# One product with the unit matrix replaced by a subtraction on GpSimd, and a new order of all steps, in a local attention with a gated feed-forward kernel

## The chip, the cores and the metric

One core of one Trainium2 chip runs the whole program. The metric is the device time of one execution in microseconds (us), and the lower the better. The kernel before took 375.93 us, the median of three runs (375.56 to 376.45). For this kernel a difference of under about 0.2%, some 0.75 us, can't be told from none.

## The reference

The input is `q`, `k`, `v` of 4 batches, 8 heads, 768 positions and 64 features, in float32. The positions are cut into 24 chunks of 32. Each chunk of queries sees 8 memory keys and its own neighbourhood:

```python
for c in range(nc):
    l_start, r_end = max(0, c_start - 16), min(S, c_end + 8)
    k_full = np.concatenate([mem_k, k[:, :, l_start:r_end]], axis=2)
    v_full = np.concatenate([mem_v, v[:, :, l_start:r_end]], axis=2)
    scores = scale * np.matmul(q_c, k_full.transpose(0, 1, 3, 2))
    a = np.exp(scores - np.max(scores, axis=-1, keepdims=True))
    a = a / (np.sum(a, axis=-1, keepdims=True) + 1e-09)
    out[:, :, c_start:c_end] = np.matmul(a, v_full)
```

The result, 4 x 768 x 512, goes through a feed-forward block whose gate mixes positions:

```python
h = gelu_tanh(x @ w_in)                      # 512 -> 1024
u, v = h[..., :512], h[..., 512:]
v_n = (v - mean(v)) / sqrt(var(v) + 1e-06) * g_ln
v_s = np.einsum('ts,bsd->btd', w_sg, v_n) + b_sg[None, :, None]
return x + (u * v_s) @ w_out
```

## The kernel before, in words

**High and low parts.** Every float32 factor of the large products is split into a part `hi`, which TensorE takes as it is, and a rest `lo = value - hi`. A product is then three products: lo times hi, hi times lo, hi times hi. The weights arrive as 64-bit words; `weight_steps` turns one piece of 128 x 512 into float32 in steps `r` (transfer, SyncE), `d3` (ScalarE), `d2`, `d5`, `d6` (VectorE), rounds it to `hi` in `d8` (ScalarE) and makes `lo` in `d9`. For most pieces `d9` is a subtraction on GpSimd (or VectorE). For the pieces of `w_in` named in `BY_TENSOR`, TensorE makes it: step `X` multiplies the piece by the unit matrix and subtracts `hi` by a product with the negative unit matrix, and `d9` is then a copy out of PSUM on ScalarE. The pieces are named by half and row block: `i10` to `i13` make the second half of `w_in` (for `v`), `i00` to `i03` the first (for `u`).

**Stages.** An attention unit `u` (24 of them, 6 for each batch, 128 positions each) is loaded by `q`, `k`, `v` (SyncE), scored by `S` (TensorE), and goes through `mx` (row maxima, VectorE), `sb` (subtract them, VectorE), `ex` (exp, ScalarE), `z` (clear absent keys, GpSimd), `sm` and `sr` (sum, reciprocal, VectorE), `nm` (normalise, VectorE or, starred, GpSimd), `T` (transpose, TensorE), `p` (copy out of PSUM, ScalarE or, starred, VectorE), `A` (times the values, TensorE), `xc` and `xh` (ScalarE) and `xl` (VectorE or GpSimd), which leave the unit's hi and lo part. Then `V` (batch, unit) multiplies by the second half of `w_in`, and `U` (batch, half, block) by the first, each with three times four or more matmuls. `v1`, `u1` are the gelu, `v5`, `vx`, `vy`, `v6`, `v7` the normalisation; `W`, `O` are the gate product and `w_out` for batches 0 and 1. Batches 2 and 3 use a form with fewer products, with steps `M` and `N`, whose weights (sums of blocks of `w_sg`, made earlier and kept in device memory by `ys`) come back by `yr` and `yq` into room that the attention buffers held before.

**The order.** Nothing loops: the text `ORDER` names every step once, and each step issues its instructions on its engine in the place where it stands there. So `ORDER` fixes the instruction stream of each of the five engines; an engine takes its own stream strictly in turn, and semaphores hold an instruction until its operands are there and its buffer is free. A star chooses a step's second engine. `zz8` and `zz4` are matmuls with the unit matrix whose result nobody reads. Four PSUM buffers `mma` to `mmd` are handed out in the order in which they come free (`mms`), to `X`, `T`, `V`, `U`, `W`, `O`, `M` and `N` alike. In the trace all helpers record one line, L107, so one reads by buffer names: `ea` to `ed` hold the scores of four units, `pt` the transposed ones, `paira` and `pairb` hi and lo of the two halves of a batch, `ma` to `mh` the weight pieces while they are made (`mb` is i11, `mf` i01, `mg` i02, `mh` i03), `raw` what was loaded for them.

At the start TensorE runs, in step names: `zz8 S0 zz4 S1 Xi10 zz8 S2 T0 S3 Xi12 T1 A0 Xi11 S4 Xi13 A1 T2 S5 T3 V01 A2 V00 S7 S6 V02 U000`.

Of the kernel before, what the change touches and what calls it, by code (L numbers as in the profile page):

```python
# [39 lines left out]
ri00 zz4 d6i10 mx0 S1 k3 q3 d3i12 d2i12 d5i12 d8i10 Xi10 sb0 mx1 sb1 ex0 v0 ri02 q4 k4 zz8 v1 z0 sm0 sr0 nm0 d6i12  # L40
d3i03 ex1 d2i03 S2 sm1 T0 d9i10 d3i00 S3 p0* sr1 nm1* d2i00 mx2 mx3 sb2 sb3 d8i11 d8i12 Xi12 d9i12 T1 A0 Xi11 ex2 q5
k5 ex3 S4 d3i02 d8i13 xc0 p1 xh0 Xi13 d9i13 d5i00 sm2 sr2 d6i00 mx4 nm2* q6 sm3 sr3 d5i03 sb4 A1 d9i11 xh1 v2 ri01 T2
S5 q7 k7 xl1 d6i03 k6 d8i00 d8i03 p2 ex4 xl0 mx5 d3i01 nm3* T3 V01 A2 ro0 V00 v5 d9i00 sb5 d2i02 d5i02 d9i03* d2i01
xh2 ex5 S7 v100 d5i01 d6i02 d6i01 d8i01 xl2 d8i02 xc1 d9i01* S6 z5 v101 sm5 sm4 v3 g00 v501 vx01 sr5 mx6 p3* sr4 vy01
d3o0 xc2 k9 V02 d2o0 sb6 d9i02 mx7 sb7 q9 nm5* ex6 U000 v601 v4 v701 nm4* T5 A3 U002 xc3 p5 T4 g50 g20 g10 S9 k11 v6
ex7 v500 g40 g21 k8 xh3 v801 A5 z6 p4 vx00 vy00 sm7 sm6 v901* v102 u1002 ga50 v600 v700 A4 xc4 xc5 v800 v502 xl3 sr6
d5o0 d6o0 xh5 v900* gb50* xl5* U003 V03 d8o0 xh4 xl4* ga20 ga00 vx02 vy02 d9o0* u1000 ga40 gb40* V05 ga10 v103 ga21
v503 v105 nm6* v602 mx9 vx03 gb20 U001 v505 vy03 sb9 ex9 sm9 v702 vx05 V04 gb00 gb10 v603 q8 ro2 g31 g30 q11 g11 T6
v703 ga30 gb30* sr7 nm7* vy05 p6* cg S11 g41 S8 ro1 ga31 u1001 v605 v705 q10 v802 U010 mx8 v803 v902 v104 u1003 ga11
k10 gb21 v504 vx04 vy04 v604 v704 sb8 v805 v905* v903* gb11 v804 v904 U012 U011 T7 S10 A6 p7* sr9 d3o1 u1010 gb31* cb  # L50
u1012 d3o2 ex8 xc6 ga41 mx11 d2o1 d5o1 W003 d2o2 sb11 d5o2 nm9* d6o1 k12 g51 W001 W002 ga51 ex11 w1003 w2003 k13 w3003
d8o1 v9 mx10 w1001 gb41 w4003 gb51 w1002 sb10 w2002 sm8 q12 q13 g01 W000 w1000 d6o2 d9o1* sr8 w2000 ga01 gb01 W012
w1012 ro3 d3o3 d2o3 d5o3 w2012 w2001 v7 T9 d8o2 ex10 w3002 w3000 z11 nm8* d6o3 S13 S12 k15 q14 q15 v8 k14 A7 xc7 u1011
mx12 W010 w4002* T8 d8o3 w4000 W011 d9o2* w1010 sb12 w2010 sm11 p9* sr11 sm10 w1011 w2011 mx13 sb13 U013 w3001 w4001
d9o3 ea1 ex12 u1013 p8 ea2 sr10 ex13 nm10* ea3* eh1 O003 O001 nm11* sm13 o1001 w3010 w4010 el1* O000 O002 v10 yl000
yl010 yl110 yl100 yc10 o1000 eb1 es1 eb2* o1003 xh7 eh2 xh6 w3012 w3011 ed1* xl7* T11 S14 S15 W013 w1013 w4012* w2013
T10 A9 p11* A8 w4011 V11 p10 xc8 el2 xl6* V10 mx14 w3013 v111 xh8 xc9 w4013 O012 xl8 es2 z12 v110 v511 sr13 o1002 ed2
mx15 v510 o1012 nm13* sm12 sr12 vx10 vy10 eh4 el4 O010 O011 sb15 nm12* vx11 sb14 vy11 v611 v711 v811 v911 v610 yc30*
ex15 v710 o1010 yc20* T12 k17 v12 k16 v11 A11 A10 o1011 ec1 ec2 ex14 sm14 sr14 p12* v810 es4 q16 v13 q17 V12 O013 v112
v512 sm15 ec3* xc10 xc11 eh3 xh10 U102 U101 u1102 xl10 el3 T13 S17 S16 V14 xh11 v910* o1013 sr15 nm15* xl11* xh9 vx12  # L60
vy12 mx17 sb17 k18 xl9* q18 es3 v14 V15 v612 v114 p13 v514 mx16 v712 out002 v812 T15 A13 A12 v115 yc40* v912 yh50 vx14
vy14 v515 ym50 p15* sb16 v614 V13 ys50 out012 k19 out003 q19 out000 ex16 v113 U111 U100 U103 vx15 vy15 nm14 v714 v615
v715 v815 u1101 v915 v513 vx13 yh60 yh40 v814 vy13 v613 v914* yl001 v713 ym40* yh70 T14 S19 S18 mx18 u1111 U113 ym70
v813 u1103 ys70 ys40 v913 sb18 ex17 ex18 u1100 W101 u1113 ym60 W111 W103 v15 yl011 z17 p14* w1101 w2101 mx19 sm17
w3101 w1103 W102 ys60 out001 w4101 w1111 k20 yl111 sr17 w2111 sm16 w2103 yc11* yc31* sr16 yc21 sb19 nm16 yh71 ym71*
W113 yh61 xc12 w3103 ex19 nm17* yh51 U110 z18 sm18 u1110 ym51 q20 k21 q21 yl101 w1102 w2102 w3102 w4102* U112 out011
ys51 w3111 xc13 W100 w1100 w2100 u1112 sr18 w1113 w2113 w3113 w4103* nm18 yc41* T17 S20 S21 W112 w1112 w2112 mx20 mx21
W110 sm19 w1110 w2110 w4113* T16 yl002 q22 k22 ys71 yh41 w3112 w3100 sb20 w3110 w4111* sb21 sr19 nm19 A15 A14 ym61 q23
yl012 out013 ym41 yr50 w4112 w4100 O100 p17 o1100 O101 O102 w4110 O103 xh12 xc14 o1101 p16* O111 O113 o1111 out010
xc15 ex21 out100 yl112 v17 yl102 v16 o1102 T18 A17 A16 O110 out101 v18 ys41 k23 ys61 xh13 yc12* yh52 xh14 xl14* ex20  # L70
sm20 yc32* yc22* yc42* ym52 yh62 o1103 out103 out102 ys52 sr20 p18* yh42 xc17 sm21 ym62* xl12 T19 p19* nm20* o1110
o1113 S22 S23 O112 mx22 xl13* o1112 V20 T20 ys62 v19 xc16 xh16 ym42* A19 A18 ys42 out111 yr51 V22 xh17 sb22 xl16* ex22
yh72 ym72 ys72 sm22 V21 xc19 xh15 sr21 nm21* xl15 v122 xl17 V24 v20 out113 v22 out110 yr52 v121 v522 db* v521 vx21
vy21 vx22 v124 vy22 v622 mx23 v120 v722 v520 V23 v21 vx20 vy20 v721 T21 p21* sb23 v524 v620 out112 v123 xc18 v523 sr22
ex23 U203 V25 p20 v720 nm22 vx23 v723 U202 v621 vz20 vz22 vy23 z23 vz21 v125 u1202 vx24 vy24 sm23 T22 A21 u1203 A20
xc20 v525 vx25 sr23 p22* v725 sh21 v624 v724 vz24 xc21 nm23* v623 vy25 v625 vz25 vz23 U213 U211 T23 A22 p23 v23 A23
yr71 yr60 c12 sl21* U201 u1201 sh22 u1213 c32 sh25 u1211 yr62 yr61 er4 yr70 c22 U200 u1200 sh26 sl26 M210 sl22* M221
M211 yr72 c42 mr211 mr210 M220 sl25 mr220 M261 M260 mr221 sh27 mr261 M251 sl27 md21 mr251 w2201* mr260 md20* w2200
# [808 lines left out]
```

## Time and profile before

| | |
|---|---|
| median of three runs | 375.93 us |
| the profiled execution | 375.81 us |
| its span, first to last instruction | 374.0 us |
| mean granted TensorE clock | 0.989 of full speed |
| busy: TensorE, VectorE, ScalarE, GpSimd | 361.4, 259.2, 179.1, 148.1 us |

The profiled execution lies 0.12 us below the median, and 1.81 us of it lie outside the span. An engine's busy time says little by itself here: TensorE is at work nearly all the time, so the places to read are the few in which it waits, and what it waits for. The rows below come from the page, from the list of who waited for whom, from the timeline of single engines, and from the list of what touched one buffer.

### The profile page before, as it was taken

The numbers are of one execution on the slowest core, as the hardware profiler recorded it, in microseconds if no ns is written. First come the engines' busy times: TensorE is split into PE (matmuls) and PEld (weight loads), VectorE is DVE, ScalarE is ACT, GpSimd is POOL, SyncE is SP. The second block draws the span as 40 slices with busy tenths as digits, with TensorE's granted clock in tenths as the row PEclk, the third lists the DMA queues.
The fourth block names the chain that finished last, engine by engine and source line by source line (L and its number), as shares of the span: only waits on it lengthen the run. The fifth ranks groups of instructions, "written<-read, shape, count | busy, mean of one in ns | idle before, by whom it ended". The sixth has DMA issues, their size and how long they took to land.

```text
span 374.0 us, 11057 instructions
## 1 busy us (share of the span) xinstructions
PE 361.4 (97%) x4762; PEld 333.3 (89%) x4762; DVE 259.2 (69%) x474; ACT 179.1 (48%) x306; POOL 148.1 (40%) x160
## 2 busy tenths in 40 slices
PE   4989999999999999999999999999999999999995
PEld 1457998999999998999999998899999889999995
DVE  3988986886874676644558281845355986988896
ACT  3556797563644382681711633674133543533340
POOL 1031434743255656453224525221825525115161
PEclk9799999999999999999999999999999999999999
DMA  7978867481913523765237969115528030224005
GB/s 296 381 274 309 320 206 230 116 271 78 328 66 119 219 86 122 244 243 174 70 87 237 340 227 336 50 58 159 198 83 268 27 87 1 86 84 147 2 0 189
DMA packets 30496, 63.76 MB, mean 170 GB/s; under 512 B 3568, under 2 KB 16624, under 8 KB 30448
## 3 DMA queue, kind: packets, MB, share of 16 engines
q1 hardware_dynamic: 30448, 63.06, 49.7%
...
q14 instruction: 11, 0.09, 0.1%
...
## 4 chain that ended last, share of the span: by engine, by line
PE 92%; DMA 3%; DVE 1%; issue 1%; SPq 1%; ACT 0%; DVEq 0%; ACTq 0%
PE mma L107 26%; PE mmc L107 21%; PE mmb L107 19%; PE mmd L107 15%; PE av L107 7%; PE s L107 4%; DMA qa<-in_qs 2%; DMA qb<-in_qs 1%; SPq L107 1%; DVE pt L107 0%; DVE vn L107 0%; DVE stats L107 0%; DVE rda L107 0%; ACT eb L107 0%; ACT vn L107 0%
## 5 line engine op out<-in xcount | busy, mean ns | idle before, releaser
L107 ACT ACT_TABLE_LOAD x24 | 30.8, 1283 | 7.0 <-DVE ec L107 2.6
L107 ACT CAST vh<-vn 128x768 fp32r<-128x768 f32 (+1 forms) x26 | 19.0, 738 | 26.2 <-PE mmd L107 10.5
L107 POOL TENSOR_TENSOR vh<-vn,vh 128x512 fp32r<-128x512 f32 (+1 forms) x11 | 17.2, 1569 | 32.7 <-ACT vh L107 32.6
L107 DVE BATCH_NORM_STATS2 stats<-vn 128x6 f32<-128x512 f32 x24 | 16.4, 688 | 18.7 <-ACT vn L107 18.6
L107 POOL TENSOR_TENSOR stats<-stats,mhalf 128x1 f32<-128x1 f32 x24 | 15.5, 648 | 28.3 <-DVE stats L107 28.3
L107 PE MATMUL mma<-w_sg_hi,vh 128*128 128x384 f32 x102 | 21.5, 337 | 0.0
L107 DVE TENSOR_TENSOR vh<-vn,vh 128x768 fp32r<-128x768 f32 (+1 forms) x15 | 16.3, 1098 | 4.6 <-ACT vh L107 4.6
L107 PEld LDWEIGHTS mma<-w_sg_hi,vh 128*128 128x128 f32 x102 | 17.9, 188 | 0.1
L107 PE MATMUL mmb<-w_sg_hi,vh 128*128 128x384 f32 x66 | 13.8, 336 | 0.8 <-DVE pt L107 0.8
L107 PEld LDWEIGHTS s<-ka,qa 64*32 64x32 f32 x704 | 8.2, 109 | 7.0 <-issue 6.5
L107 PE MATMUL s<-ka,qa 64*32 64x64 f32 x704 | 10.0, 232 | 4.5 <-DMA qa<-in_qs 4.0
L107 PE MATMUL mmc<-w_sg_hi,vh 128*128 128x384 f32 x66 | 13.9, 337 | 0.0
L107 DVE TENSOR_SCALAR vn<-vn,stats 128x512 f32<-128x512 f32 x12 | 9.5, 791 | 5.1 <-POOL stats L107 5.0
L107 PEld LDWEIGHTS mmb<-w_sg_hi,vh 128*128 128x128 f32 x66 | 11.6, 188 | 0.9 <-DVE pt L107 0.9
L107 PEld LDWEIGHTS s<-kb,qb 64*32 64x32 f32 x768 | 8.7, 109 | 3.9 <-issue 1.8
L107 PE MATMUL mmd<-w_sg_hi,vh 128*128 128x384 f32 x54 | 11.6, 335 | 0.0
L107 PEld LDWEIGHTS mmc<-w_sg_hi,vh 128*128 128x128 f32 x66 | 11.5, 188 | 0.1
L107 DVE SCALAR_TENSOR_TENSOR mma<-mma,g_all,b_all 128x384 f32<-128x384 f32 x6 | 3.8, 626 | 11.2 <-PE mma L107 11.2
L107 PE MATMUL s<-kb,qb 64*32 64x64 f32 x768 | 10.6, 232 | 0.8 <-DMA qb<-in_qs 0.8
L107 ACT ACTIVATE vn<-mmc 128x512 f32<-128x512 f32 x8 | 4.8, 597 | 13.7 <-PE mmc L107 11.8
L107 PE MATMUL mma<-pairb,w_in_hi 128*128 128x384 f32 x56 | 10.9, 335 | 0.0
L107 PE MATMUL mma<-w_sg_lo,vh 128*128 128x384 f32 x51 | 10.6, 335 | 0.0
...
## 6 DMA issues: line engine op xcount, KB each, us to landing
...
```

The source lines that it names most:

```text
L107: return self.tc.keep_in_program_order(getattr(self.engine, name)(*args, **kw))
```

## The change

One name leaves the list of pieces whose low part TensorE makes, so that the low part of piece `i11` becomes a GpSimd subtraction `w_in_lo<-mb,w_in_hi`; step `Xi11`, with its three matmul records, and the copy out of PSUM on ScalarE are gone. All steps of `ORDER` stand in a new order, of which two lines are shown:

```diff
-BY_TENSOR = ("i10", "i11", "i12", "i13")
+BY_TENSOR = ("i10", "i12", "i13")
...
-ri11 d3i11 d2i11 d5i11 ri10 d3i10 d2i10 d6i11 k0 zz8 ri13 d5i10 q0 d3i13 S0 k1 q1 ri12 d2i13 d5i13 d6i13 ri03 k2 q2
+ri11 ri13 d3i13 d3i11 d2i13 d5i13 d6i13 zz8 d2i11 d5i11 d6i11 d8i11 ri10 q0 q1 k0 q2 ri00 d3i10 S0 mx0 sb0 d2i10 d5i10
```

TensorE's stream now begins: `zz8 S0 zz4 S1 zz8 T0 S2 S3 Xi10 A0 T1 Xi12 A1 Xi13 S4 S5 T2 V00 T3 A2 V01 S6 S7 V02 U003`.

The first transfers on SyncE, in the order of issue, before (`raw` buffers are pieces of `w_in`; the two `vn` are keys and queries of unit 2):

```order
L107 DMA rawb<-in_w_in 128x1024
L107 DMA rawa<-in_w_in 128x1024
L107 DMA ka<-in_ks 128x736
L107 DMA rawd<-in_w_in 128x1024
L107 DMA qa<-in_qs 128x512
L107 DMA kb<-in_ks 128x736
L107 DMA qb<-in_qs 128x512
L107 DMA rawc<-in_w_in 128x1024
L107 DMA rawh<-in_w_in 128x1024
L107 DMA vn<-in_ks 128x736
L107 DMA vn<-in_qs 128x512
L107 DMA rawe<-in_w_in 128x1024
```

and with the change:

```order
L107 DMA rawb<-in_w_in 128x1024
L107 DMA rawd<-in_w_in 128x1024
L107 DMA rawa<-in_w_in 128x1024
L107 DMA qa<-in_qs 128x512
L107 DMA qb<-in_qs 128x512
L107 DMA ka<-in_ks 128x736
L107 DMA vn<-in_qs 128x512
L107 DMA rawe<-in_w_in 128x1024
L107 DMA rawh<-in_w_in 128x1024
L107 DMA kb<-in_ks 128x736
L107 DMA rawc<-in_w_in 128x1024
L107 DMA rawf<-in_w_in 128x1024
```

After these come, before, `kb` and `qb` of unit 3; with the change first the keys of unit 2 (`vn`), then `qb` and `kb` of unit 3. So seven pieces of `w_in` stand ahead of unit 3's operands where six stood, and unit 1's keys `kb` stand behind five pieces where they stood behind three.

VectorE around the lo parts of units 0 and 1, which are the two rows `paira<-av,paira` (`rda<-ed` is the sum for unit 3), before:

```order
L107 TENSOR_REDUCE mxb<-s 128x8
L107 TENSOR_REDUCE rda<-ed 128x8
L107 RECIPROCAL rda<-rda 128x8
L107 SCALAR_TENSOR_TENSOR mh<-rawh,mh 128x512
L107 TENSOR_TENSOR ea<-s,mxb 128x4x128
L107 TENSOR_TENSOR paira<-av,paira 128x4x128
L107 SCALAR_TENSOR_TENSOR mh<-rawh,mh 128x512
L107 TENSOR_TENSOR paira<-av,paira 128x4x128
```

and with the change:

```order
L107 TENSOR_TENSOR paira<-av,paira 128x4x128
L107 TENSOR_REDUCE rdc<-ec 128x8
L107 RECIPROCAL rdc<-rdc 128x8
L107 TENSOR_SCALAR mg<-mg 128x512
L107 SCALAR_TENSOR_TENSOR mg<-rawg,mg 128x512
L107 TENSOR_TENSOR paira<-av,paira 128x4x128
L107 TENSOR_REDUCE rda<-ed 128x8
L107 RECIPROCAL rda<-rda 128x8
L107 COPY pt<-mmc 128x4x128
```

The sum for unit 3 now stands behind both lo parts and behind two steps on piece i02 (`mg`). GpSimd in the same place, before:

```order
L107 MEMSET ea 32x4x2x16
L107 TENSOR_TENSOR eb<-eb,rdb 128x4x128
L107 TENSOR_TENSOR ec<-ec,rdc 128x4x128
L107 TENSOR_TENSOR ed<-ed,rda 128x4x128
L107 TENSOR_TENSOR w_in_lo<-me,w_in_hi 128x512
L107 MEMSET eb 32x4x2x8
```

and with the change:

```order
L107 MEMSET ea 32x4x2x16
L107 TENSOR_TENSOR ea<-ea,rda 128x4x128
L107 TENSOR_TENSOR eb<-eb,rdb 128x4x128
L107 TENSOR_TENSOR w_in_lo<-mb,w_in_hi 128x512
L107 TENSOR_TENSOR ec<-ec,rdc 128x4x128
L107 TENSOR_TENSOR w_in_lo<-mf,w_in_hi 128x512
L107 TENSOR_TENSOR w_in_lo<-mh,w_in_hi 128x512
L107 TENSOR_TENSOR ed<-ed,rda 128x4x128
```

The new subtraction for `mb` stands ahead of unit 2's normalisation `ec`, and two more, for i01 and i03, stand between those of units 2 and 3.

On SyncE, where the blocks for `M` come back once the attention buffers are free (the name ending in 6 before, and 1 with the change, is the second of the two block buffers), before:

```order
L107 DMA block_3516<-kept 128x2x384
L107 DMA block_3515<-kept 128x2x384 x3
L107 DMA w_out_hi<-kept_o 128x2x256
L107 DMA w_out_lo<-kept_o 128x2x256
L107 DMA block_3516<-kept 128x2x384 x2
```

and with the change:

```order
L107 DMA block_3510<-kept 128x2x384
L107 DMA block_3511<-kept 128x2x384
L107 DMA w_sg_hi<-kept 128x384
L107 DMA w_sg_lo<-kept 128x384
L107 DMA block_3510<-kept 128x2x384 x2
L107 DMA block_3511<-kept 128x2x384
```

The third transfer for the first block buffer, which was fourth in the row, is now sixth. On TensorE the steps between the last attention step `A23` and the first product with that buffer were `U201 U200 M210 M221 M211 M220` and are now `U201 M210 M211 U213 M220`.

## Rows read from the trace of the kernel before

**Rows 1.** The page: span, TensorE's busy time, the chain that ended last.

```profile
span 374.0 us, 11057 instructions
PE 361.4 (97%) x4762; PEld 333.3 (89%) x4762; DVE 259.2 (69%) x474; ACT 179.1 (48%) x306; POOL 148.1 (40%) x160
...
PE 92%; DMA 3%; DVE 1%; issue 1%; SPq 1%; ACT 0%; DVEq 0%; ACTq 0%
```

**Rows 2.** Who TensorE waited for: us in total, times, longest.

```profile
PE s L107 <- DMA qa<-in_qs: 4.0, 1, 4.0
PE mma L107 <- POOL mhalf L107: 1.4, 1, 1.4
PE s L107 <- DMA qb<-in_qs: 0.8, 1, 0.8
PE mmb L107 <- DVE pt L107: 0.8, 1, 0.8
PE av L107 <- issue: 0.7, 1, 0.7
PE s L107 <- issue: 0.5, 1, 0.5
PE mmd L107 <- DVE pt L107: 0.5, 1, 0.5
```

**Rows 3.** Busy us by stretch (start:end; length; PE PEld DVE ACT POOL; clock; DMA share; GB/s).

```profile
10.00:20.00 10.00, 9.20 (x206) 4.97 (x207) 8.93 (x18) 5.15 (x9) 0.94 (x2) 0.77 1.00 379
```

**Rows 4.** The chain of waits in order of time: start, us, what.

```profile
13.48 5.40 DMA qb<-in_qs
...
22.65 1.28 PE mma L107 x3
...
30.11 0.59 PE mmd L107 x4
...
...
34.55 2.95 PE mma L107 x12
```

**Rows 5.** TensorE's timeline: S3, V01, V02, and U201 behind A23.

```profile
19.02 0.85 PE L107 MATMUL s<-kb,qb 64*32 64x64 f32 x64 [0.81 <-DMA qb<-in_qs]
...
30.46 1.19 PE L107 MATMUL mmb<-w_in_hi,paira 128*128 128x512 f32 x4
...
38.86 1.20 PE L107 MATMUL mmc<-w_in_hi,paira 128*128 128x512 f32 x4
...
254.51 0.96 PE L107 MATMUL mmd<-paira,w_in_lo 128*128 128x384 f32 x4
```

**Rows 6.** VectorE's, GpSimd's and ScalarE's timeline at the start.

```profile
18.31 0.68 DVE L107 COPY pt<-mmb 128x512 f32<-128x512 f32 x1
...
20.51 0.68 DVE L107 TENSOR_REDUCE mxa<-s 128x8 f32<-128x512 f32 x1
21.11 0.68 DVE L107 TENSOR_TENSOR ec<-s,mxc 128x512 f32<-128x512 f32 x1
...
24.51 0.58 ACT L107 COPY pt<-mmd 128x512 f32<-128x512 f32 x1
...
26.92 0.64 DVE L107 SCALAR_TENSOR_TENSOR mh<-rawh,mh 128x512 int32<-128x512 int32 x1
27.15 1.31 POOL L107 TENSOR_TENSOR ed<-ed,rda 128x512 f32<-128x512 f32 x1 [1.87 <-DVE rda L107]
...
29.96 1.28 POOL L107 TENSOR_TENSOR w_in_lo<-me,w_in_hi 128x512 fp32r<-128x512 f32 x1 [1.49 <-ACT w_in_hi L107]
30.00 1.78 DVE L107 SCALAR_TENSOR_TENSOR mh<-rawh,mh 128x512 uint32<-128x512 uint32 x1
```

**Rows 7.** The fourth block transfer, and the matmuls that read blocks (first and last start).

```profile
L107 SPq DMA_DIRECT2D block<-kept x1: 612/612/612, 256.7 to 256.7; - x1
DMA to landing us min/median/max: 6.8/6.8/6.8
...
L107 PE MATMUL mma<-block,vh x27: 332/337/340, 265.0 to 278.5; 128*128 128x384 f32 x27
```

More of the change, by code (lines that the diff above doesn't have):

```diff
@@ L38 @@
 ORDER = """
-ri11 d3i11 d2i11 d5i11 ri10 d3i10 d2i10 d6i11 k0 zz8 ri13 d5i10 q0 d3i13 S0 k1 q1 ri12 d2i13 d5i13 d6i13 ri03 k2 q2
[L40 to L78, printed above, removed]
@@ L94 @@
-out300 out311 th340 th341 tl341 tl331 N370 nr370 N371 tl340 N321 nr371 ns370* ns371* out313 out312 ns340* N340 nr321
-out301 nr340 ns341 N341 nr341 out302 out303
+ri11 ri13 d3i13 d3i11 d2i13 d5i13 d6i13 zz8 d2i11 d5i11 d6i11 d8i11 ri10 q0 q1 k0 q2 ri00 d3i10 S0 mx0 sb0 d2i10 d5i10
+ex0 ri03 z0 d3i03 k1 sm0 d2i03 ri12 d3i12 d6i10 sr0 d5i03 ri01 k2 zz4 nm0* S1 mx1 q3 zz8 d3i00 d2i12 sb1 k3 d5i12 ex1
+d3i01 d8i10 d8i13 sm1 d6i12 d2i01 d6i03 T0 v0 d5i01 d6i01 sr1 d2i00 p0* d8i12 d8i01 S2 v1 ri02 k4 S3 Xi10 A0 q5 mx2
@@ new lines @@
+sb2 mx3 xh0 d5i00 nm1* d9i11 q4 k5 T1 p1 d8i03 Xi12 d9i10 ex2 A1 Xi13 d6i00 d8i00 sb3 xl0 ex3 g40 g10 v2 g00 d9i13
+d3i02 S4 sm2 sr2 q6 S5 k7 d9i12 xh1 xc0 d2i02 d5i02 xl1 sm3 sr3 nm2* d9i01 T2 p2* mx5 q7 V00 v100 g31 mx4 sb5 ex5 sb4
+v500 d9i03 nm3* k6 T3 p3 d6i02 ro0 g20 g50 ex4 g41 A2 V01 xh2 d8i02 d9i00* xl2 vx00 vy00 S6 S7 mx7 d9i02 k9 v101 sb7
+sm4 v3 q9 v600 z5 ex7 ga40 v5 V02 U003 U002 k8 q8 sm5 v700 d3o0 sr4 v501 d2o0 mx6 d5o0 vx01 vy01 sb6 v4 S9 xc1 ga00
+ga20 v800 A3 v900 ex6 z6 v601 v102 mx9 sr5 nm5* ga50 d6o0 U000 S8 T5 xc3 xh3 ga10 sm6 v502 nm4 gb50* u1000 xc2 p5 gb40
@@ new lines @@
+w2000 W002 W001 nm8* g01 d3o2 w1002 w2002 w3002 w4002* d2o2 d3o3 d5o2 sm9 d2o3 w3000 d6o2 ga01 T8 gb01 d8o2 d8o1 p8
+S12 yl010 w1001 d5o3 S13 yc10 W003 w2001 w1003 w2003 w3003 u1010 mx12 d6o3 d8o3 d9o3* d9o1* w4000* mx13 sr9 nm9 d9o2*
+sb12 q14 W012 w1012 W011 w2012 U011 w3001 u1011 xc6 nm10* ea1* ea2 ea3 eh1 w3012 W010 k14 v8 v9 T9 S14 A8 eb1* ex12
+w4012* el1 es1 p9* A9 w1010 w1011 mx14 sb13 yl110 v10 k15 v11 q16 v12 eb2 w4001* w4003* w2010 z12 sm12 W013 w1013
+w2013 w2011 xc9 ex11 w3011 O000 T10 w4011* O002 sr12 p10* w3013 z11 xc8 eh2 O003 O001 ed1* w4013 o1002 sb14 o1000 sm11
@@ new lines @@
+T19 S22 out102 ys72 S21 o1113 mx21 mx22 xl17 xl15* p19* out101 ys62 k23 out110 sb21 V20 V23 ex21 T20 A18 A19 sb22 ex22
+v120 V25 out100 xc19 v123 V24 v125 p20 v122 yr52 v21 q23 out113 sm21 sr21 v520 vx20 nm21 v523 sm22 sr22 v522 vx22
+xl13* vy22 v622 v722 nm22* T21 v22 out111 vy20 v720 vx23 v723 vz22 xc18 v124 er4 S23 U200 V21 v121 U202 v620 T22 mx23
+v525 sb23 ex23 v521 vx21 vy21 vx25 z23 vy25 A20 p21 A21 v621 v625 v725 p22* vz20 v721 sm23 U203 out112 u1200 vz21 U212
+v23 vz25 xc21 sh21 xc20 sr23 nm23* v524 vx24 v724 vy23 v623 vz23 vy24 T23 A22 p23* A23 yr62 yr70 yr50 sl21* u1212
@@ new lines @@
+u1202 u1203 U201 M210 M211 U213 v624 vz24 sh22 xc23 c12 c32* sl22* u1201 c22 c42 sh26 sl26* mr210 M220 sh25 sl25*
+mr220 yr60 yr61 M260 M221 u1213 mr211 mr260 mr221 sh27 sh24 sl27* M261 w2201* sh23 xc22 w3201 yr71 er2 yr72 M250 mr261
+sl24 M271 M251 md21* mr271 w4201* mr251 mt21 md20 w2200* w3200 w4200 sl23 mr250 U210 M270 mr270 mt20 yr42 yr41 yr40
+M241 N210 nk20 M240 er1 yq70 nr210 mr241 w2213 M231 w2212* w2203* w3203 w4203 mr240 w2202 w3202 N211 mr231 nk21 nr211
+w4202 U211 w3213 u1211 w4213* M230 N220 mr230 yq71 w2211* N221 nr221 nr220 w3212 w4212 xh20 u1210 xh18 xl20* t121*
@@ new lines @@
+v735 ns241 N241 nr241 ns240* sl31* vz33 u1301 vz35 U312 U310 c13 sh32 yq61 M310 sl32* u1302 u1310 u1312 c33 c23 c43
+sh36 sl36* mr310 M321 N240 sh35 sl35* M311 M320 mr311 mr321 mr320 nr240 M361 mr361 sh37 sl37 md31 M360 U313 u1313
+mr360 sh34 sh33 out213 sl34* U303 M370 M350 sl33* out211 out210 out203 yq42 out201 out202 M330 md30 w2300* w3300
+w4300* w2301 u1303 mr350 mr370 mt30 mr330 w2312 w2310 t130 w3301 w4301 t330* M371 M351 mr351 mr371 mt31 yq41 U311
+out212 yq40 th310 w3312 tl310* w2313 u1311 w3313 M331 w4312* t230 mr331 w4313* w2311 M340 M341 mr340 t131 w2302 t331
@@ L96 @@
+th311 mr341 w3302 th331 N311 N310 nk31 w4302* N331 w2303 tl311* t430 t231 nr331 w3303 N351 N330 w4303* nr311 tl331
+N321 th321 nk30 th320 nr351 nq31 nr310 nr330 nr321 N350 t431* tl320 tl321* N320 nr350 nq30 nr320 th330 th340 N361
+nr361 ns361* out300 N360 nr360 tl340 tl330 N371 nr371 ns360* N370 ns371* nr370 ns341* th341 tl341 N341 out310 out313
+out311 out301 ns370* out312 nr341 out303 N340 ns340* nr340 out302
 """
```

40 lines of the change are left out of this document (25 added, 15 removed).

## The prediction

> **What bounds the kernel now.** I read the page first: TensorE is busy for 361.4 of 374.0 us, and the chain that ended last is 92% TensorE [rows 1]. So the time is TensorE's work plus the places where it stands, and the second view, who TensorE waited for, lists all of them: seven waits, 8.7 us [rows 2]. Five of them (4.0, 1.4, 0.8, and 0.7 and 0.5 put down to "issue") lie in the first 30 us, where operands are still arriving. The last two, 0.8 and 0.5 us for a copy into `pt` by VectorE, come at about 75 and 66 us. From there to the end TensorE never waits. A change can therefore gain by shorter TensorE work only where TensorE isn't waiting for something else, and lose wherever the new order brings an operand late.
>
> In the first 30 us the third and fourth views say who sets the pace. From 10 to 20 us the transfer engines are full (share 1.00, 379 GB/s) and VectorE is busy for 8.93 of 10 us [rows 3]; the chain of waits has the transfer of `qb` from 13.48 on [rows 4], for which S3 starts only at 19.02 [rows 5]. TensorE becomes the bound behind S3.
>
> **What goes.** `Xi11` is 1.28 us of TensorE [rows 4], and a copy of some 0.6 us on ScalarE. What comes is one GpSimd subtraction of 1.28 us, as the row of the same form shows [rows 6]. Taken alone, that is a gain of up to 1.28 us, 0.3%. Whether it arrives depends on the order.
>
> **The start, up to V02.** V02 is the first step ahead of which the two orders have done the same work, but for `Xi11`; behind it both do the same. So the start is worth the shift of V02, which began at 38.86 [rows 5].
>
> S3 first. Its operands now follow seven pieces of `w_in` instead of six. Half a megabyte more at 379 GB/s [rows 3] is 1.4 us, so S3 starts at about 19.02 + 1.4 = 20.4.
>
> From S3 to V01 TensorE took 30.46 - 19.02 = 11.44 us [rows 5], with three `X` steps, three transposes and the two issue gaps of 1.2 us together [rows 2]. From S3 to V00 it now has three `X` steps too: `Xi11` is gone, but `Xi10`, which stood ahead of S3 where TensorE had time, has come behind it. It has two transposes, since T3 (0.59 [rows 4]) now follows V00. That is 10.85 us with the gaps, 9.65 without. V00 starts at 31.25 or 30.05. So the 1.28 us is spent within the start. VectorE agrees with this pace and no earlier one: the copy of unit 0 into `pt` was its 22nd compute step, at 18.31, and is the 28th; six steps at the pace of 0.60 of the rows at 20.51 and 21.11 put it at 21.9, its end at 22.6 [rows 6], when S3 and `Xi10` have just ended (20.4 + 0.85 + 1.28).
>
> From V01 to V02 it was 8.40 us [rows 5] without a transpose; now it is 8.40 + 0.59 from V00, so V02 would start at 40.2 with the gaps, 39.0 without, if T3 finds its operand.
>
> T3 is where the new subtraction bites. Its normalisation on GpSimd (`ed`, 1.31 [rows 6]) waits for the sum of unit 3 on VectorE, which now stands behind two steps on piece i02 (`mg`) and the lo part of unit 1. VectorE reaches them about nine steps behind the copy, near 27.6; but the first needs ScalarE, which takes piece i02 only after copying the product `Xi13` out of PSUM, at 27.8 to 29, so the two steps start at 29.0 to 30.2. GpSimd from 27.6 on has unit 2's normalisation and two subtractions, 1.31 + 2 x 1.28: until 31.5. The row at 30.00 shows what then happens: the same form of VectorE step that took 0.64 alone took 1.78 beside GpSimd's subtraction of 29.96 to 31.24 [rows 6]. One step held costs 1.1 us. With both on `mg` held, they end at 32.5; lo part, sum and reciprocal (0.6 + 0.6 + 0.2) make 33.9, the normalisation 35.2. T3 would start at 35.2, while V00 ends at 33.0 to 34.2 (2.95 long [rows 4]). V02 then starts at 35.2 + 0.59 + 5.45 = 41.2. With none held T3 comes at 33.0 and costs nothing.
>
> So the start is worth between +0.1 (no gaps, nothing held) and +2.4 us (both held). I take +1.3: the issue gaps return, as they stood here [rows 2], and T3's wait is mostly hidden by them.
>
> The Trainium skill (SBUF — State Buffer, section "SBUF: two separate sides") says that GpSimd and VectorE hold a shared port pair as an exclusive lock, for a whole instruction, and that a VectorE instruction with two SBUF inputs or in a two-port mode waits for it. The row of 1.78 us agrees. By the rule both steps on `mg` are held and the start costs the full +2.4; by the row, which has one held step, half of it. A step that reads PSUM, as `pt` copies do, is by the same rule not held, so that the harm stays with T3.
>
> **The rest of the program.** The two waits for copies into `pt`, 1.3 us together [rows 2], hang on VectorE being late, behind exp and its sum. In the new order T7 and T6 stand in front of two score steps, and their copies ahead of the sums that wait for exp, so I take most of it as gone: -1.0, with 0 and -1.3 as its ends; TensorE also comes later there, which gives VectorE time.
>
> New is a tight place at `T5 T4 A5`: A5 needs T5's copy by ScalarE, 0.58 [rows 6], and has only T4 (0.59) over it; before, a score step stood there too. With a hand-over on either side of the copy I take +0.2, between 0 and 0.7.
>
> Then the blocks for `M`. Before, the fourth transfer, issued at 256.7, landed 6.8 us later, at 263.5, and the first product with it ran at 265.0, 1.5 us later [rows 7]; from the end of the last attention step, 254.51 [rows 5], these are 9.0 and 10.5. Now one `M` step less stands before that product (9 matmuls, some 1.56), so it is due at 8.9, and the transfer it needs stands two half-size transfers further back: 384 KB, 1.0 us at the rate above [rows 3]. The first of the row may go a step earlier, since its room is free before the last attention step. I take +0.4, between 0 and 1.1.
>
> The closing stretch of `N` steps has the same products in another sequence, and the last two of them are followed by the same adds and one transfer: 0.
>
> **The sum.** The profiled execution took 375.81, with 1.81 outside its span. +1.3 - 1.0 + 0.2 + 0.4 = +0.9 gives 376.7; it lay 0.12 below the median of the runs, so 376.8 is my figure for the median.
>
> **Rivals.** (1) No change. The gaps at the start don't return and one step on `mg` is held, so that the start costs 0.5; blocks in time; the `pt` waits half gone: 375.93 + 0.5 - 0.6 + 0.1 = 375.9. For it: gaps of "issue" are no part of the order. Against it: VectorE and the transfers have more in front of V00 than before.
> (2) Faster. VectorE gets its steps on `mg` in front of GpSimd's subtractions, the first of which starts at 27.6 + 1.31 = 28.9, T3 follows V00 at once, and TensorE runs without a gap from S3 on; all `pt` waits vanish and no new one comes: 375.93 + 0.1 - 1.3 + 0.1 = 374.8. For it: the waits that vanish are real rows, and behind 75 us nothing has waited. Against it: `Xi10` behind S3.
> (3) Much slower. Both steps on `mg` are held and the sixth transfer lands 1.1 us late: 375.93 + 2.4 - 1.0 + 0.2 + 1.1 = 378.6.
>
> **How the numbers follow.** The forecast has 0.36, no change 0.30, faster 0.25, much slower 0.09. What can be told from no change is 0.2%, 0.75 us: below 375.2 is faster, above 376.7 slower. The forecast lies just above that edge; of its 0.36, which runs by itself from 376.3 to 377.6, some 0.05 fall within it, and rival 3 adds 0.09: slower 0.41, same 0.34, faster 0.25. The range that leaves out a tenth on either side goes from 374.8 to 378.2.
>
> **What would show it.** Right: S3 at 20 to 21 us; V02 between 39.5 and 41; a VectorE step on `mg` of over 1.2 us beside a `w_in_lo` subtraction; T3 among the waits with GpSimd's `ed` behind it; no `pt` wait at 60 to 80 us; at most 1 us of waiting for `block`. Wrong: V02 at or before 38.9, or a wait of over 1 us in the stretch between 80 and 250 us, of which I have assumed none.

## The result and the profile after

The changed kernel takes 381.54 us (381.20 to 381.96), the kernel before 375.93: a ratio of 1.0149, with a 95% interval of 1.0123 to 1.0174. The forecast was 376.8 with a range up to 378.2. The sign was the likeliest of the three, the size is far off.

The page of the profiled execution (381.20 us by its own time), with the row of the instruction queue, to which I had paid no heed before:

```profile
span 379.4 us, 11044 instructions
PE 363.1 (96%) x4759; PEld 333.2 (88%) x4759; DVE 261.9 (69%) x482; ACT 178.1 (47%) x306; POOL 142.0 (37%) x150
...
q8 instruction: 37, 0.61, 0.6%
...
PE 76%; DVE 12%; DMA 3%; issue 3%; ACT 2%; SPq 1%; POOL 1%; DVEq 0%; ACTq 0%; POOLq 0%
```

Against [rows 1], TensorE's share of the chain has fallen from 92 to 76%. It has three records fewer, but 1.7 us more of busy time: its granted clock fell to 0.50 (1.2 GHz) while it waited for S0's operands and stayed there from 8.3 to 18.5 us, in the kernel before from 7.7 to 14.6 us. Behind that both have 1.00 (2.4 GHz) up to TensorE's last product. Who TensorE waited for (us in total, times, longest):

```profile
PE s L107 <- DMA ka<-in_ks: 4.2, 1, 4.2
PE s L107 <- issue: 3.6, 3, 1.5
PE mma L107 <- POOL mhalf L107: 1.4, 1, 1.4
PE s L107 <- DVE ma L107: 0.8, 1, 0.8
PE av L107 <- DVE pt L107: 0.5, 1, 0.5
PE av L107 <- issue: 0.4, 2, 0.2
PE mmd L107 <- DVE xd L107: 0.4, 1, 0.4
PE mmd L107 <- DMA block<-kept: 0.4, 1, 0.4
PE mma L107 <- DVE pairb L107: 0.3, 1, 0.3
PE av L107 <- ACT pt L107: 0.2, 1, 0.2
```

Of [rows 2] the two waits for `pt` behind 60 us are gone, as forecast. The rows put down to "issue" have grown from 1.2 to 4.0 us. TensorE's timeline shows where (start, us, operation, count of records, idle time before). Here and below a row that reaches over the end of the stretch asked for is cut there, so that S3, with 64 records, shows 43. First the kernel before, then the changed one:

```profile
24.59 0.64 PE L107 MATMUL s<-ka,qa 64*32 64x64 f32 x40 [0.49 <-issue]
...
28.44 0.30 PE L107 MATMUL av<-pt,vb 64*64 64x32 f32 x3 [0.66 <-issue]
```

```profile
19.58 0.66 PE L107 MATMUL s<-kb,qb 64*32 64x64 f32 x43
...
22.24 1.14 PE L107 MATMUL av<-pt,va 64*64 64x32 f32 x64 [0.53 <-DVE pt L107]
...
24.98 0.30 PE L107 MATMUL av<-pt,vb 64*64 64x32 f32 x4
...
27.86 0.86 PE L107 MATMUL s<-ka,qa 64*32 64x64 f32 x64
30.21 0.86 PE L107 MATMUL s<-kb,qb 64*32 64x64 f32 x64 [1.49 <-issue]
...
34.26 0.60 PE L107 MATMUL mma<-ident,ed 128*128 128x128 f32 x4
...
39.46 0.49 PE L107 MATMUL s<-kb,qb 64*32 64x64 f32 x30
41.15 0.51 PE L107 MATMUL s<-kb,qb 64*32 64x64 f32 x34 [1.19 <-issue]
41.58 1.20 PE L107 MATMUL mmc<-w_in_hi,paira 128*128 128x512 f32 x4
...
49.66 0.58 PE L107 MATMUL s<-kb,qb 64*32 64x64 f32 x36 [0.88 <-issue]
```

Against [rows 5], S3 comes 0.56 later (19.58 for 19.02), V02 2.72 later (41.58 for 38.86), and TensorE's last product ends 5.22 later (375.29 for 370.07). I compared every TensorE step by the time from its start to the next step's start, behind V02:

| place | us against before | what it is in the trace |
|---|---|---|
| up to V02 | +2.72 | S3 +0.56, A0's wait for `pt` +0.53, issue gaps 2.91 in place of 1.15 |
| A6, S8 | -0.94, -0.52 | the two `pt` waits gone |
| U002 | +0.90 | S9 waits; its `qb`, issued at 42.71, took 6.9 us to land |
| A4 | +0.51 | an issue gap of 0.21 and what it draws after it |
| V20, N351, N350 | +0.54, +0.54, -0.26 | waits for `pairb` and `xd` |
| M260 | +0.65 | wait for `block` |
| T4 | +0.31 | A5 waits for T5's copy |
| some 190 others | +0.77 | none above 0.2 |

Between S3 and V02 both kernels do the same TensorE work, `Xi10` standing in the place of `Xi11`, so the waits alone explain this stretch.

**What an issue gap is.** Counting TensorE's records, products and weight loads both, the gap inside A1 and the one ahead of S5 are 254 apart (60 products of A1, three of `Xi13`, 64 of S4, each with its load), and from there to the gap inside S7 it is 508. In the kernel before, the two gaps are 254 apart too. The page counts 37 packets of instructions for TensorE's 9,518 records, one for 257. Asking the transfer view for ever narrower stretches places each packet. From 27.8 to 27.9 us of the changed kernel (queue, packets, MB, share of the engines):

```profile
q1 hardware_dynamic: 27, 0.04, 112.2%
q8 instruction: 1, 0.02, 60.0%
```

S5 starts 2.3 us behind this packet. The packets at 23.3 and 38.6 stand 2.3 and 2.6 us ahead of the ends of the gaps in A1 and S7; before, those at 22.2 and 25.7 stood 2.4 and 2.7 ahead of the ends of its two gaps. And a packet follows each boundary: 2.3 us behind the one at 25.52, 1.1 behind the one at 30.21. By these rows a block is asked for when TensorE enters the one ahead of it, its packet queues behind the data, and TensorE can go on some 2.4 us behind the packet. If the 254 instructions in hand are used up sooner, TensorE stands. This was theory A; its rivals were a data or buffer wait that the profile misses, and the subtraction itself by its lock on VectorE.

### The profile page after: what moved, and what is told of

Its sections match the earlier page's. It is cut to its first block, busy times and chain, and to the rows that moved or that the text cites. A ratio compares the mean times of both kernels' runs of the same rounds, so it can differ in the third digit from the quotient of the medians.

```text
span 379.4 us, 11044 instructions
## 1 busy us (share of the span) xinstructions
PE 363.1 (96%) x4759; PEld 333.2 (88%) x4759; DVE 261.9 (69%) x482; ACT 178.1 (47%) x306; POOL 142.0 (37%) x150
## 4 chain that ended last, share of the span: by engine, by line
PE 76%; DVE 12%; DMA 3%; issue 3%; ACT 2%; SPq 1%; POOL 1%; DVEq 0%; ACTq 0%; POOLq 0%
PE mmc L107 18%; PE mmd L107 18%; PE mma L107 15%; PE mmb L107 15%; PE av L107 6%; PE s L107 4%; DMA block<-kept 2%; DMA ka<-in_ks 2%; SPq L107 1%; DVE pairb L107 1%; DVE vn L107 1%; DVE xc L107 1%; ACT pairb L107 1%; DVE w_out_lo L107 1%; DVE paira L107 1%
## 5 line engine op out<-in xcount | busy, mean ns | idle before, releaser
L107 POOL TENSOR_TENSOR vh<-vn,vh 128x512 fp32r<-128x512 f32 (+1 forms) x8 | 13.0, 1626 | 22.9 <-ACT vh L107 22.9
L107 PE MATMUL mma<-w_sg_hi,vh 128*128 128x384 f32 x78 | 16.7, 334 | 0.0
L107 PE MATMUL mmc<-w_sg_hi,vh 128*128 128x384 f32 x72 | 15.2, 336 | 0.0
L107 PE MATMUL mmb<-w_sg_hi,vh 128*128 128x384 f32 x72 | 14.6, 337 | 0.0
L107 PE MATMUL mmd<-w_sg_hi,vh 128*128 128x384 f32 x66 | 14.0, 334 | 0.0
L107 ACT ACTIVATE vn<-mmd 128x512 f32<-128x512 f32 x9 | 5.4, 601 | 18.3 <-PE mmd L107 18.3
L107 PEld LDWEIGHTS mma<-w_sg_hi,vh 128*128 128x128 f32 x78 | 13.8, 188 | 0.0
L107 PE MATMUL mmd<-w_in_hi,paira 128*128 128x512 f32 x48 | 13.2, 397 | 0.0
L107 PE MATMUL mmc<-w_in_hi,pairb 128*128 128x512 f32 x48 | 13.1, 396 | 0.0
L107 POOL TENSOR_TENSOR vn<-vn 128x512 fp32r<-128x512 f32 (+1 forms) x5 | 8.0, 1590 | 12.3 <-ACT vn L107 9.1
L107 ACT ACTIVATE vn<-vn,stats 128x512 f32<-128x512 f32 x12 | 8.5, 723 | 8.3 <-POOL stats L107 6.7
```

The source lines that it names most:

```text
L107: return self.tc.keep_in_program_order(getattr(self.engine, name)(*args, **kw))
```

## The experiments

**The two halves of the change, apart.** First the named change in the order of before:

```diff
-BY_TENSOR = ("i10", "i11", "i12", "i13")
+BY_TENSOR = ("i10", "i12", "i13")
-... T1 A0 Xi11 ex2 q5
+... T1 A0 ex2 q5
```

> The order of before with only the named change in it: Xi11 is left out and GpSimd subtracts the low part in the place of ScalarE's copy. Theory A (the new order costs the time, the subtraction does not; TensorE's gaps without a releaser are instructions that arrive late, at a fixed number of TensorE instructions): 1.28 us of TensorE goes, part of it comes back in the two early gaps, which grow since TensorE reaches them sooner; 374.8 to 375.9 us, gap places shifted by the six instructions of Xi11. Theory B (the subtraction on GpSimd, beside VectorE's work, costs the time): 377 us or more.

376.66 us against 375.72, ratio 1.0022 (1.0005 to 1.0039): between the two theories, and no gain. Where the 1.28 us went is in TensorE's rows:

```profile
22.06 0.30 PE L107 MATMUL s<-ka,qa 64*32 64x64 f32 x4
24.23 0.82 PE L107 MATMUL s<-ka,qa 64*32 64x64 f32 x60 [1.86 <-issue]
24.98 2.08 PE L107 MATMUL mma<-md,ident 128*128 128x512 f32 x2
```

Before, this gap stood behind the first product of S4; now it is behind the fourth, six records later, which are those of `Xi11`. TensorE came to the boundary sooner and stood there longer: 1.86 for 0.49. V02 started at 39.67, 0.81 later than before, and everything behind it took as long as before (0.04 us more). The gaps aren't all of it in this profile: S3 came 0.91 sooner than before, so from S3 to V02 it lost 1.72 us and the product's 1.28. The gaps took 1.18 of these 3.0 us. Another 1.15 are `Xi13`, the row at 24.98, which took 2.43 us to the next step in place of 1.28: from 24.9 to 28.4 us, just behind the gap, the granted clock was at 0.50. The clock doesn't make the loss by itself, since the three executions of the twelve with a mean granted clock of 1.000 took 376.46 to 376.62.

The new order, with the product kept:

```diff
-BY_TENSOR = ("i10", "i12", "i13")
+BY_TENSOR = ("i10", "i11", "i12", "i13")
-... S3 Xi10 A0 q5
+... S3 Xi10 Xi11 A0 q5
```

> The new order, with Xi11 kept as a product on TensorE behind Xi10 and copied by ScalarE. Theory A (the order is the cause): 381 to 383 us, as the changed kernel or up to 1.3 more. Theory B (the subtraction is the cause): 376 to 378 us.

382.95 against 375.72, 1.0184 (1.0132 to 1.0236): the order carries the loss. The gaps have moved by the six records of `Xi11`, to behind the 61st product of S4 and the 27th of S7, and V02 starts at 41.28, no later than without the product: by these two profiles 1.28 us of TensorE work cost nothing here.

```profile
29.85 0.30 PE L107 MATMUL s<-ka,qa 64*32 64x64 f32 x3 [1.34 <-issue]
...
40.72 0.63 PE L107 MATMUL s<-kb,qb 64*32 64x64 f32 x37 [1.04 <-issue]
```

**The boundary, moved.** In the changed kernel, behind the first warming products:

```diff
-... d6i13 zz8 d2i11
+... d6i13 zz8 yy16 d2i11
+            for _ in range(int(name[2:])):
+                tensor.matmul(bank[0:CH, 0:64], ident[0:64, 0:CH], ident[0:64, 0:64], start=True, stop=True)
```

> The changed kernel with 16 tiny products on the unit matrix (64 TensorE instructions by the records' count) in the time before S0, when TensorE waits for data anyway. Theory A (instructions come in blocks of some 254, and the gap stands at the boundary): the gap of 1.49 us ahead of S5 goes, and one of about that size stands inside S4, some 32 of its 64 matmul records earlier than its end at most; the gap of 1.19 us behind the 30th record of S7 moves to the very start of S7 or the end of S6; the 0.23 inside A1 moves ahead of A1. Time 381.0 to 382.2. Rival (an operand or a buffer that the profile doesn't show holds S5 and S7): both gaps stay where they are, ahead of S5 and behind the 30th record of S7.

386.03 against 375.72, so the time was missed by 4 us, but the places were hit: the gap ahead of S5 stands behind the 32nd record of S4 (0.67 us and not 1.5), that of S7 ahead of the last of S6.

```profile
29.23 0.46 PE L107 MATMUL s<-ka,qa 64*32 64x64 f32 x32
30.35 0.45 PE L107 MATMUL s<-ka,qa 64*32 64x64 f32 x31 [0.67 <-issue]
...
40.12 0.84 PE L107 MATMUL s<-ka,qa 64*32 64x64 f32 x63
42.61 0.24 PE L107 MATMUL s<-ka,qa 64*32 64x64 f32 x1 [1.65 <-issue]
```

A hidden operand can't do that: S5 and S7 start without a wait. The time rose since S6 now ended late; the loads of unit 9 wait for S7, and S9 stood 2.01 us for `qb`.

**Fewer transfers ahead of the blocks.**

```diff
-... ex3 g40 g10 v2 g00 ... V00 v100 g31 ... ro0 g20 g50 ex4 g41
+... ex3 v2 ... V00 v100 ... ro0 ex4
-... v3 q9 v600 ... ga40 v5
+... v3 q9 g40 g10 g00 g31 g20 g50 g41 v600 ... v5
```

> The changed kernel with the seven early loads of w_sg (192 KB each) moved behind q9 in SyncE's queue, and the ScalarE step that reads the first of them moved with them; TensorE's order is untouched. Theory A (instruction blocks wait behind queued transfers): the gaps of 1.49 us ahead of S5 and 1.19 us in S7 are together at least 1.2 us smaller, at the same places; 379.3 to 380.5 us. Rival (a hidden operand or buffer, or VectorE's steps): the gaps stay within 0.3 us, 381 us or more.

382.21 against 375.72, 1.0168: the time was missed. The gaps did what theory A said: 0.65 ahead of S5, none in A1 or S7, V02 at 39.57, 2.01 sooner. More than that was lost at S8, whose `q8` now stood behind the seven loads and behind those of unit 9. In the changed kernel SyncE had issued unit 8's loads first (from 39.7 us, unit 9's from 41.7), although `ORDER` names unit 9's first: SyncE's stream is to be read from the trace, not from `ORDER`.

```profile
28.73 0.48 PE L107 MATMUL s<-kb,qb 64*32 64x64 f32 x33 [0.65 <-issue]
...
38.79 0.85 PE L107 MATMUL s<-kb,qb 64*32 64x64 f32 x64
...
53.86 0.85 PE L107 MATMUL s<-ka,qa 64*32 64x64 f32 x64 [2.73 <-DMA qa<-in_qs]
```

To mend that, the loads went behind those of units 8 and 9, and the steps that use them (`ga40 gb40 ga00 gb00* ga20 ga50 gb50* ga10`) to ahead of `ga41`.

> The changed kernel with the same seven loads of w_sg moved back as in the run before, but now behind every load of the units 8 and 9, and the eight steps that make hi and lo parts of them moved behind unit 4 and 5's work; TensorE's order is untouched. Theory A (instruction blocks queue behind transfers): the gap ahead of S5 at most 0.7 us, none inside S7, V02 at about 39.6 (41.58 in the changed kernel), S9's wait of 0.88 gone or smaller, no wait of 2.7 us ahead of S8 as in the run before; own time of the profiled execution 378.3 to 379.5 (381.20 in the changed kernel). Rival (the early gaps cost nothing in the end, since what follows is held by something else): 380.5 or more although V02 is early.

388.77 against 376.09: a failure of the design. Those steps, waiting for the late loads, now stood ahead of unit 4's low part on VectorE, and V04 waited 4.75 us for `pairb`. The early part is a second sample: 0.69 ahead of S5, none in S7.

The other direction, in the kernel before:

```diff
-... q5
-k5 ex3 S4
+... q5
+k5 g00 g50 g20 g10 g40 ex3 S4
```

> The kernel before with five of its later w_sg loads (192 KB each, 0.96 MB) moved forward in SyncE's queue to stand behind the loads of unit 5; every other engine's order is untouched, and nobody needs those tiles sooner. Theory A: the early gaps of TensorE (0.49 in S4, 0.66 in A1) grow, together by 0.7 to 2 us, at the same instruction counts, and a gap in S7 or S6 can appear; 376.5 to 378 us. Rival (gaps are set by operands or by VectorE): no gap grows but the one whose operand lands later; within 0.5 us of before.

376.60 against 376.09, 1.0016 (0.9995 to 1.0037). The gaps grew at their places, from 0.49 and 0.66 to 0.76 and 0.93, and one of 0.42 came in the score step ahead of V02: +0.96, and V02 0.72 later. The time agrees, but doesn't tell it from nothing, and neither does the growth, as the next run shows.

**The forecast's best term, alone.** The kernel before, with `p6*` made `p6` behind `ga30`, and `p7*` put ahead of `v905* v903*`:

> The kernel before with the two copies into pt for which TensorE waited at 66 and 75 us made earlier: that of unit 6 by ScalarE, that of unit 7 by VectorE ahead of two subtractions. This is the term of the prediction that was to gain 1.0 us, by itself. If it was right: both waits gone, U010 some 0.5 us and W003 some 0.7 us sooner against the step before them, 374.6 to 375.2 us. Rival (another wait takes their place): 375.7 or more.

375.67 against 376.09, 0.9992 (0.9965 to 1.0018). Both `pt` waits are gone (A6 -0.84, S8 -0.53 against before), and T7 has grown by 0.74, since S10 now waits for VectorE's step on `ea`:

```profile
75.70 0.48 PE L107 MATMUL s<-ka,qa 64*32 64x64 f32 x33 [0.67 <-DVE ea L107]
```

This profile also shows how much the gaps vary by themselves. Up to 60 us its program is that of before, yet its gaps were 1.17 (S4), 0.61 (A2) and 1.50 (ahead of V02), together 3.28 in place of 1.15, and V02 started at 41.39 in place of 38.86. It is one of its kernel's three longest executions, 377.91 us where the median is 375.67; the times run from 374.61 to 378.90. So one execution tells the place of a gap, but not its size.

**S5 behind V00.** In the changed kernel `S5` goes behind `V00`:

```diff
-... q6 S5 k7 ... p2* mx5 q7 V00 v100
+... q6 ... p2* V00 S5 mx5 k7 q7 v100
```

> The changed kernel with S5 moved behind V00 on TensorE alone, so that a step of 24 instructions and 2.9 us stands where 128 instructions of 0.8 us stood ahead of the boundary. Theory A: the gap of 1.49 us goes and no other of over 0.7 us comes before V00 ends; V00 starts 2 us or more sooner; V01 1 to 1.5 us sooner; the gap in S7 stays between 0.8 and 1.8; own time 379.7 to 380.5. Rival (S5 waited for its own buffer or data, or VectorE sets the pace): V01 within 0.4 us of 35.85 and the time 381 or more.

384.24 against 376.09: the time was missed, and the edit doesn't do what was meant. Counted in records, the boundary that stood ahead of S5 now stands ahead of T2; V00, the slow step, is behind it. And there the gap is, 1.33 us long. The view puts it down to `ec`, but GpSimd had ended `ec` at 30.14, 0.59 us before T2 started, and T2 started 2.3 us behind an instruction packet (28.4), as the steps at the other gaps do. So the gap didn't go (without it T2 would have stood some 0.8 us for `ec`), and the run is one more sample of its place. V00 was 0.33 sooner (in a profile with S3 0.56 later), and S6 waited 2.26 us for `ka`, whose load had moved back with unit 7's.

```profile
30.73 0.60 PE L107 MATMUL mmc<-ident,ec 128*128 128x128 f32 x4 [1.33 <-POOL ec L107]
...
41.73 0.46 PE L107 MATMUL s<-ka,qa 64*32 64x64 f32 x33 [2.26 <-DMA ka<-in_ks]
```

**S9's wait.** Only SyncE's queue changes: in the trace it is now `k8 q8 k9 q9 v3 v4` in place of `k8 q8 v4 k9 v3 q9`.

> The changed kernel with one thing moved: on SyncE's queue the loads of unit 9 (kb, qb) go ahead of those of v3 and v4, and that of v4 last, so qb of unit 9 has 1 MB less ahead of it; every other engine's order is the same. Theory C (S9's 0.88 us was its qb, queued too late): S9's wait at most 0.3 us, U002 to S9 some 0.7 us shorter, the early gaps unchanged (1.49 and 1.19 within 0.5), time 0.5 to 1.0 under the changed kernel's in the same call. Rival (S9 waits for an instruction block or for its scores' buffer): S9's wait stays above 0.6.

381.70 against 375.78. S9 starts at 48.95 with no wait, 1.8 us behind the landing of its `qb`, and U002's term is gone; the sum behind V02 is +1.10, against +2.50 in the first profile of the changed kernel. In the profile of the changed kernel beside it S9 still started with the landing of its `qb` (49.5 us), but stood for only 0.1 us, since V02 had come at 42.21, and the sum was +1.93. So the queue sets when S9 can start; what that is worth differs from execution to execution. The times, 381.70 (380.00 to 383.91) and 382.71 (381.25 to 384.15), overlap.

**Loads and q9 together**, with `g40 g00 g20` behind `q7` and `g50 g10 g41 g31` behind `v4`:

> The run before, and of the seven early loads of w_sg only the three that ScalarE reads first stay early, behind q7; the other four go behind v4. No other step moves. Theory A (instruction blocks queue behind transfers): the gap ahead of S5 under 0.9 us, that in S7 under 0.7, V02 0.8 to 2 us sooner than in the changed kernel, and the time 1.3 to 2.8 us under the changed kernel's in the same call: 378.5 to 380. Rival (the gaps' time is taken back by waits that they cover, as in the run with S5 moved, where a wait for the normalised scores came out from under the gap): V02 sooner by under 0.5 us.

381.34 against 375.78. The rival held: the gap ahead of S5 is gone and V01 starts at 35.95, against 36.09 in the changed kernel beside it, for T3's wait has come out (here `ed` did end last, at 34.24).

```profile
34.30 0.66 PE L107 MATMUL mma<-ident,ed 128*128 128x128 f32 x4 [1.20 <-POOL ed L107]
...
41.81 0.51 PE L107 MATMUL s<-kb,qb 64*32 64x64 f32 x34 [1.74 <-issue]
```

**The changed kernel again.**

> The changed kernel itself once more, as the measure for the two runs beside it: 381.0 to 382.5 us, gaps at the same TensorE instructions (behind the 4th record of A1, ahead of S5, behind the 30th of S7) with sizes that may differ by some tenths.

382.71 against 375.78, 1.0170 (1.0133 to 1.0208), with gaps of 0.53, 1.64 and 1.58 at the same three places.

**S7's block, then both early chains.** In the first, `v5 g50 g41` move from ahead of S7 to behind `v3` (`k8 q8 k9 q9 v3 g50 v4 v5 g41`). In the second `g10 g31` go there too, `g00` behind `q7`, and `sm3 sr3 nm2* nm3*` ahead of `d2i02 d5i02 xl1`.

> The changed kernel with SyncE's queue alone changed: the loads of unit 9 ahead of v3, v5 and two of the w_sg loads (1.0 MB together) from ahead of S7 to behind v4. So the block of instructions that S7 needs finds an emptier queue; the three w_sg loads ahead of S5's block stay. Theory A: the gap ahead of S5 stays (1.3 to 1.7), that in S7 (1.2 to 1.7 in the changed kernel) falls under 0.5, V02 at 40.4 to 41.2 against 41.6 to 42.2, S9 without a wait; the time 1 to 2.2 us under the changed kernel's 382.71: 380.5 to 381.7. Rival (the gap in S7 isn't set by what is queued): it stays over 1.0.

> The run before, and both chains that end ahead of V01 shortened: of the w_sg loads only two stay ahead of unit 7's, and VectorE sums unit 3 ahead of the two steps on piece i02, GpSimd normalises it ahead of two low parts of w_in. Theory A with the wait under the gap: gap ahead of S5 under 0.8, T3 without a wait, gap in S7 under 0.6; V02 at 39.0 to 40.0; time 2.5 to 3.8 us under the changed kernel's 382.71: 378.9 to 380.2. Rival (a third chain comes out): V02 at 40.5 or later.

381.02 and 381.50 against 376.22. The first came out as expected: S7's gap is gone, S5's stays (1.35), and V02 is at 41.19, since S6 waited 0.71 for `ka`. In the second T3 has no wait and S7's gap is 0.47, but S5's is 1.36 although one load is left ahead of it: V02 at 40.82, a miss. Both keep the late losses (V20, N351, M260, A4). All profiles of the changed kernel's TensorE order with the boundaries in their places:

| loads of `w_sg` and `v5` | gap ahead of S5 | gap in S7 |
|---|---|---|
| as in the changed kernel (three profiles) | 1.49, 1.64, 1.35 | 1.19, 1.58, 1.04 |
| all seven behind q9 (two) | 0.65, 0.69 | 0, 0 |
| early three moved, `v5` and three kept ahead of S7 | 0 | 1.74 |
| early three kept, `v5` and two moved from ahead of S7 | 1.35 | 0 |
| one kept ahead of S5, two ahead of S7 | 1.36 | 0.47 |

All but the last 1.36 follow theory A; that one stays open. Each is one execution, but the groups lie apart: at S5's boundary 0 to 0.69 with the early loads moved, against 1.33 to 1.64 in six profiles that kept them all (those with `Xi11` and with S5 moved among them); the run with the boundary moved, whose blocks hold other steps, had 0.67. The times alone would not have told these versions apart: but for the 388.77, they run from 1.0125 to 1.0170 against before, and their intervals overlap. No version of the new order had a median under 381.0 us. So the runs show what makes the gaps; that taking them away gives the time back they don't show, for each time something else came to hold TensorE.

**The clock.** The waits' list leaves one thing out. Between 23 us and TensorE's last product, five of the profiles have a stretch in which the granted clock was at 0.50 (1.2 GHz), each shortly behind a wait of TensorE: 24.9 to 28.4 us (the named change alone), 53.7 to 57.1 (the boundary moved), 54.8 to 58.2 and 66.9 to 70.3 (the two runs with the loads behind `q9`), and 43.2 to 46.6 (loads and q9 together, where V02 took 1.59 us more than before; that execution, 383.06, was the slowest of its six). Other waits of that length have none behind them, as the 2.26 us ahead of S6 with S5 moved. In the profiles of the kernel before and of the changed kernel there is no such stretch, so it's no part of the difference told above.

**Room for the named change.** The order of before without `Xi11`, and `ri02` moved from behind `v0` to behind `k5`, `d3i02` to behind `xh1`; then the same with the two copies made earlier.

> The named change alone in the order of before (as the first run), and besides it the load of w_in's piece i02 moved behind those of unit 5, ScalarE's first step on it behind unit 1's cast. So half a megabyte less is queued when TensorE asks for the block that S4 stood 1.86 us for. Theory A: that gap falls to 0.2 to 0.9, and the gain of Xi11 comes through in part: 374.8 to 375.8, at or under before. Rival (the gain is lost to something else): 376.3 or more, as the first run.

> The run before with the two copies into pt made earlier as in the run with two copies. If both gains come through: 373.8 to 375.0, under before. Rival: the copies bring nothing here either, within 0.4 of the run before.

375.23 and 375.18 against 376.22: ratios 0.9984 (0.9956 to 1.0011) and 0.9965 (0.9938 to 0.9992). The last is the only version whose interval lies under before, and narrowly: some 0.35%. In the first, the block's packet stands at 21.0 in place of 21.9 us, and S4's gap is 1.12 in place of 1.86, which is more than was expected; gaps of 0.66 ahead of T2 and 0.37 in S6 follow. V02 starts at 37.91, 0.95 sooner than before, but 0.72 of that lie ahead of S3, in a profile whose clock didn't fall at the start. In the second the sum behind V02 is -0.28, with S10's wait on `ea` again:

```profile
23.80 0.41 PE L107 MATMUL s<-ka,qa 64*32 64x64 f32 x25 [1.36 <-issue]
...
72.94 0.86 PE L107 MATMUL s<-ka,qa 64*32 64x64 f32 x64 [0.70 <-DVE ea L107]
```

## Why the prediction was wrong

**The steps that failed** are two. The first is "I take +1.3: the issue gaps return, as they stood here", for a start that measured +2.72. The gaps were a row without a cause, carried over at its size. They come from a queue: a gap is what is left when the next block, behind the transfers queued ahead of it, takes longer than TensorE needs for the 254 instructions in hand. The new order put A1, S4 and S5 in one row and S6 and S7 in another, each step 128 instructions in under 1.1 us, and seven loads of `w_sg` among the transfers of the same stretch. The gaps became 2.91 in place of 1.15 us, and one came where there had been none. That difference of 1.76 is one of two executions, and before's instructions showed 3.28 in another; but that one lay 2.24 us above its kernel's median, while the two compared here lie within 0.4 of theirs.

The second step is "From there to the end TensorE never waits", and with it "the same adds and one transfer: 0": behind V02 the sum had no term but for the copies, T5 T4 A5 and the blocks. What it left out came to 3.0 us, the larger part of the miss. These waits are told below from the trace; of them only S9's was tried in a run.

**S3** came 0.56 later, not 1.4, but one pair of profiles doesn't make the term over-sized. In three other profiles with before's instructions up to there S3 started at 18.11 to 18.50, not at 19.02. And in the changed kernel no operand held it: it followed S2 at once, on a TensorE whose clock had been at half until 18.5 us. In three later runs with the same first transfers, whose clock was back at 1.00 from 12.4 to 19.2 us, S3 waited 1.8 us for `kb`, until 19.4 or 19.5. So the transfer came 0.4 to 1.4 later, depending on which of before's four starts one takes. **A0** waited 0.53 where the working had the copy just in time.

**T3** was worked out in the right way, and hidden. Of the two steps on `mg` the first, at 29.14, took 0.61 us beside `ec`'s normalisation and wasn't held; the second was held; and `ed` ended at 34.06, between the bounds of 33.0 and 35.2:

```profile
29.79 1.64 DVE L107 SCALAR_TENSOR_TENSOR mg<-rawg,mg 128x512 int32<-128x512 int32 x1
```

```profile
29.43 1.45 POOL L107 TENSOR_TENSOR w_in_lo<-mf,w_in_hi 128x512 fp32r<-128x512 f32 x1
...
33.02 1.04 POOL L107 TENSOR_TENSOR ed<-ed,rda 128x512 f32<-128x512 f32 x1 [0.43 <-DVE rda L107]
```

But V00 ended there too, at 34.3, since the gap ahead of S5 had held it. So the wait had no row in the changed kernel; the run with fewer early loads brought it out at 1.20. Two chains of nearly the same length end at T3, and taking one away gains little.

**The `pt` waits** went as forecast, and were worth 1.46 where the term had 1.0. Alone in the kernel before, they gave half of it back at S10.

**T5 T4 A5** (+0.2) measured +0.31, **the blocks** (+0.4) +0.65: right, a little small. A wait of 0.36 cost 0.65: the waits' list leaves out what a product still in flight covers, so the time from start to start is the safer measure.

**Not seen:** S9's `qb` (0.90), A4 (0.51), V20 (0.54), and the tail of N steps (0.54 less 0.26) that was put at 0. "From there to the end TensorE never waits" was a row of the old order, and no promise for a new one. These make 2.23, the scattered rest 0.77. With the start's other 1.42 and 0.36 on the two terms above, less the 0.46 that the copies gave beyond theirs, that is the 4.3 us between the forecast's +0.9 and +5.2.

That the named change gains up to 1.28 by itself was wrong for the same reason as the first step: by itself it gained nothing, and with half a megabyte less queued ahead it brought some part of a microsecond at most, which its interval doesn't tell from nothing.
